# Bias rows by DMA broadcast, the index table first on Pool, and a later third batch, in a fused Fourier-mixing and channel-mix kernel

## The chip, the cores and the metric

One core of one Trainium2 chip. The metric is the device time of one execution in microseconds (us). All runs told of here are in the same, fast state (granted clock 0.995 to 1.0). In the views PE is TensorE and PEld its weight loads, DVE is VectorE, ACT is ScalarE, POOL is GpSimd, and SPq marks a DMA that SyncE issues; a bracket at the end of a line gives the engine's wait before it and what ended that wait. "Ratio" always means the mean time of one kernel's fast runs over the mean of the other's of the same rounds, so it is not quite the ratio of the medians quoted beside it; the brackets are 95% intervals.

## The reference

```python
def _attn_ref(x, w_r, w_i, b_r, b_i):          # x: (8, 3072, 256)
    X = np.fft.rfft(x, axis=1); Xr, Xi = X.real, X.imag
    Yr = Xr @ w_r - Xi @ w_i + b_r             # complex linear layer with a bias
    Yi = Xr @ w_i + Xi @ w_r + b_i
    Y  = soft_threshold(Yr, 0.01) + 1j * soft_threshold(Yi, 0.01)
    return np.fft.irfft(Y, n=3072, axis=1)

def _moe_ref(x, mu_k, mu_r, w_k, w_v, w_r):    # on the result of the first
    x_prev = x moved on by one token
    xk = mu_k * x + (1 - mu_k) * x_prev;  xr = mu_r * x + (1 - mu_r) * x_prev
    k = np.maximum(xk @ w_k, 0);  v = (k * k) @ w_v
    return sigmoid(xr @ w_r) * v
```

## The kernel before

The transform of 3072 points is split as 96 x 32, and both halves are matmuls with tables of sines that the kernel makes itself at the start (`FT`, `FI`, `G`, `GI`). A batch goes through these stages. Line numbers are those of the kernel before; in the changed kernel most are 8 to 25 lower.

- **First** transforms, L280: x against `FT`; the result goes to DRAM (`Adr`, L291) and comes back in another layout as `A` (L305). The first two batches go another way, with x turned by transposes instead (L335, L353).
- **Middle**: second transforms (L378 for group 0, L395), the complex linear layer (L423), bias and threshold on DVE and ACT, then back with `GI` (L462). The result goes to DRAM (`Vdr`, L475) and comes back as `V` (L486).
- **Last** transforms, L543: `V` against `FI`. Then the token tiles: relu units L635, gates L662, output L679.

A small scheduler in the kernel's own Python code lays the work of all batches out in one order. Every unit has a `due` time, and estimates of when its inputs are ready; of the units that are ready, the one with the lowest due time goes next to TensorE (PE).

The start:

```python
    bb, bsel = ...                                  # zeroed on DVE
    load_x(0, 0)
    bbf = ...                                       # two small loads of b_r, b_i
    nc.gpsimd.iota(n1c, ...)
    seli = scs[0:2, 600:856]...
    nc.gpsimd.iota(seli, ...)                       # L87, 2 x 256 elements
    ...                                             # bsel, bb from seli, bbf on DVE
    nc.gpsimd.iota(fmul, ...)                       # L110
    for q in range(1, 4):
        load_x(0, q)                                # L68, also on Pool (gpsimd)
    ...                                             # FT; four iotas n2c; ident
    nc.gpsimd.iota(qk, pattern=[[1, NG], [96, 32]], ...)   # L143, 128 x 768
    nc.vector.tensor_scalar(out=qk, in0=qk, scalar1=j24, scalar2=n2c, ...)  # L153
    ...                                             # 7 us of DVE work: the angles of G
    wr = load_w("wr", w_r, NCD, D)
    wi = load_w("wi", w_i, NCD, D)
```

The bias rows, spread over the partitions by two matmuls and five copies:

```python
    def table_bias(ps, h, end):
        nc.tensor.matmul(ps[:, 0:512], bsel[:, 0, :], bb.rearrange("p a d -> p (a d)"), ...)
        nc.tensor.matmul(ps[:, 512:768], bsel[:, 1, :], bb[:, 0, :], ...)
        def evac(k):
            for t_, lo in ((bias, 0), (bias, 512), (bias0, 512)):
                nc.scalar.activation(t_[:, lo:lo + 512], ps[:, 0:512], AF.Copy, ...)
            nc.scalar.activation(bias0[:, 0:256], ps[:, 512:768], AF.Copy, ...)
            nc.scalar.activation(bias0[:, 256:512], ps[:, 0:256], AF.Copy, ...)
```

The due times (P = 71.5 us is a batch's period; the code counts batches from 0, the text from one, so `b == 2` is the third batch):

```python
        else:                                       # batches 2 to 7
            fb += first(b, s - 0.9 * P, s - 0.2 * P)
            fa += middle(b, s, s + 0.5 * P)
            fc += last(b, s + 0.75 * P, s + 0.95 * P)
```

Of the kernel before, what the change touches and what calls it, by code (L numbers as in the profile page):

```python
# [22 lines left out]
def kernel(  # L23
# [41 lines left out]
    def load_x(b, q):  # L65
# [5 lines left out]
    bb = const.tile([128, 2, D], BF16, name="bb")  # L71
    bsel = const.tile([128, 2, 128], BF16, name="bsel")
    nc.vector.memset(bb, 0.0)
    nc.vector.memset(bsel, 0.0)
    load_x(0, 0)
    bbf = const.tile([2, D], FP32, name="bbf")
    nc.sync.dma_start(out=bbf[0:1, :], in_=b_r.rearrange("(o d) -> o d", o=1))
    nc.sync.dma_start(out=bbf[1:2, :], in_=b_i.rearrange("(o d) -> o d", o=1))
# [7 lines left out]
    seli = scs[0:2, 600:856].rearrange("p (a c r) -> p a c r", a=2, c=2)  # L86
    nc.gpsimd.iota(seli, pattern=[[0, 2], [1, 2], [0, 64]], base=0, channel_multiplier=1,  # L87
                   allow_small_or_imprecise_dtypes=True)
# [13 lines left out]
    for i in range(2):  # L102
        nc.vector.tensor_copy(out=bb[0:2, i, :], in_=bbf)

    nc.vector.tensor_scalar(out=bsel[0:2].rearrange("p a (c r) -> p a c r", c=2), in0=seli, scalar1=1.0,
                            scalar2=None, op0=ALU.not_equal)
    nc.vector.tensor_copy(out=bsel[0:2, 1, 64:65], in_=bsel[0:2, 1, 0:1])

# [3 lines left out]
    for q in range(1, 4):  # L112
        load_x(0, q)
# [17 lines left out]
    for r in range(4):  # L131
# [5 lines left out]
        nc.vector.memset(sc1[sl], float(2 * PI / N) if r % 2 == 1 else 0.0)  # L137
    ident = const.tile([128, 128], FP16, name="ident")
# [3 lines left out]
    qk = scr[:, 0:768].rearrange("p (g k) -> p g k", k=32)  # L142
    nc.gpsimd.iota(qk, pattern=[[1, NG], [96, 32]], base=0, channel_multiplier=0,  # L143
                   allow_small_or_imprecise_dtypes=True)
# [10 lines left out]
    for c in range(2):  # L155
# [8 lines left out]
    hk = scs[:, 500:516]  # L164
    nc.gpsimd.iota(hk, pattern=[[96, 16]], base=48, channel_multiplier=0,
                   allow_small_or_imprecise_dtypes=True)
# [24 lines left out]
    wi = load_w("wi", w_i, NCD, D)  # L191
    muk = const.tile([128, NCD], FP32, name="muk")
# [12 lines left out]
    free = {"pe": 0.0, "act": 6.0, "dve": 13.3}  # L205
# [537 lines left out]
    bias = const.tile([128, 1024], BF16, name="bias")  # L743
    bias0 = const.tile([128, 1024], BF16, name="bias0")

    def table_bias(ps, h, end):
        nc.tensor.matmul(ps[:, 0:512], bsel[:, 0, :], bb.rearrange("p a d -> p (a d)"), start=True, stop=True)
        nc.tensor.matmul(ps[:, 512:768], bsel[:, 1, :], bb[:, 0, :], start=True, stop=True)

        def evac(k):  # L750
            for t_, lo in ((bias, 0), (bias, 512), (bias0, 512)):
                nc.scalar.activation(t_[:, lo:lo + 512], ps[:, 0:512], AF.Copy, bias=0.0, scale=1.0)
            nc.scalar.activation(bias0[:, 0:256], ps[:, 512:768], AF.Copy, bias=0.0, scale=1.0)
            nc.scalar.activation(bias0[:, 256:512], ps[:, 0:256], AF.Copy, bias=0.0, scale=1.0)
            done["bias"] = run_on("act", k, 2.6)
            release(h, done["bias"])

        at(end, evac)

# [9 lines left out]
    P = 71.5  # L769
    START = 50.0  # L770
    tok, val, fa, fb, fc, tab = [], [], [], [], [], []
    for b in range(B):
# [5 lines left out]
        elif b == 1:  # L778
            fb += direct(b, 35.0, 36.0, 50.0)
            fa += middle(b, 41.0, 65.0)  # L780
            fc += last(b, s + 0.75 * P, s + 0.95 * P)
        else:
            fb += first(b, s - 0.9 * P, s - 0.2 * P)
            fa += middle(b, s, s + 0.5 * P)
            fc += last(b, s + 0.75 * P, s + 0.95 * P)
# [26 lines left out]
    done["FT"] = 5.0  # L812
    at(13.3, tables)
# [59 lines left out]
```

## Time and profile before

| | before |
|---|---|
| device time, median of 3 (range) | 595.51 us (595.29 to 595.68) |
| span of the profiled execution | 593.3 us |
| PE busy | 566.7 us, 96% |
| first L423 | 21.65 us |
| L378 of batches 2, 3, 4, 5 | 45.48, 120.91, 190.80, 261.68 us |

Second, two windows of the kernel before (window, length, then busy us of PE, PEld, DVE, ACT, POOL, the granted clock, DMA share, GB/s). The second is the worst of the steady state: 1.4 of 10 us are lost on PE.

```profile
120.00:130.00 10.00, 9.86 (x81) 7.33 (x81) 9.18 (x16) 6.77 (x8) 0.00 (x0) 1.00 0.20 54
...
250.00:260.00 10.00, 8.60 (x107) 6.84 (x106) 7.04 (x16) 6.44 (x8) 0.00 (x0) 1.00 0.81 243
```

The full timeline of that stretch, still before, says why: the last transforms of the fourth batch wait for `V`, which was stored from 234.18 us and asked for again only at 243.09.

```profile
234.18 3.48 SPq L475 DMA_DIRECT2D Vdr<-V  x4
...
243.09 1.91 SPq L486 DMA_DIRECT2D V<-Vdr  x4
...
251.19 0.34 PE L543 MATMUL banks<-FI,V 96*128 96x96 f16 x4 [0.39 <-DMA V<-Vdr]
...
252.49 1.02 PE L543 MATMUL banks<-FI,V 96*128 96x96 f16 x20 [0.96 <-DMA V<-Vdr]
```

### The profile page before, as it was taken

The page shows a single profiled execution, that of the slowest core. Times are in us where ns is not written, and L with a number is a line of the kernel's source. Part 1 is how long each engine was busy: PE and PEld are TensorE (multiplying, and loading weights), DVE is VectorE, ACT ScalarE, POOL GpSimd, SP SyncE. Part 2 cuts the span into 40 slices and gives each one's busy share as a digit, 9 for nine tenths or more (in the row PEclk, how much of TensorE's full clock was granted, in tenths as well). Part 3 has the DMA queues.
Part 4 walks back from the last instruction along what each step waited for, and adds up shares of the span by engine and source line. Part 5 has one row for each costly group of instructions (what it writes and reads, how often), then busy time and mean ns, then how long its engine had stood idle before and what let it go on. Part 6 is the DMA issues. An engine that isn't in the chain of part 4 may idle for free.

```text
span 593.3 us, 12315 instructions
## 1 busy us (share of the span) xinstructions
PE 566.7 (96%) x4824; PEld 428.9 (72%) x4891; DVE 519.3 (88%) x834; ACT 425.5 (72%) x467; POOL 23.5 (4%) x53
## 2 busy tenths in 40 slices
PE   4989999999999999999999999999999999999996
PEld 3878666777767787677777777677876787776665
DVE  7788999789998899888998989988999889979883
ACT  6887967677768677676777677777776867766652
POOL 7001000000000000000000000000000000000000
PEclk9999999999999999999999999999999999999999
DMA  8936888624599256773478655683338722362223
GB/s 150 167 80 158 186 193 226 178 72 104 129 225 237 60 139 140 204 225 67 116 167 245 154 120 129 165 238 106 100 93 235 178 55 73 103 164 72 68 57 90
DMA packets 68878, 84.06 MB, mean 142 GB/s; under 512 B 9042, under 2 KB 53844, under 8 KB 68820
## 3 DMA queue, kind: packets, MB, share of 16 engines
q1 hardware_dynamic: 62916, 68.98, 41.7%
q0 software_dynamic: 5712, 14.03, 15.1%
q8 instruction: 38, 0.62, 0.4%
q10 hardware_dynamic: 192, 0.26, 0.2%
q14 instruction: 20, 0.16, 0.1%
HBM read 50.07 MB, written 47.19 MB: 164 GB/s over the span
## 4 chain that ended last, share of the span: by engine, by line
PE 81%; ACT 7%; DVE 4%; DMA 3%; issue 2%; SPq 1%; POOL 0%; POOLq 0%; DVEq 0%; ACTq 0%
PE banks L679 27%; PE banks L635 23%; PE banks L423 14%; PE banks L662 5%; PE banks L462 3%; PE banks L280 3%; PE banks L395 3%; ACT rl L641 2%; PE banks L543 2%; ACT rg L667 1%; DMA xs<-in_x_dram 1%; DMA Adr<-A 1%; ACT YT L227 1%; PE banks L353 1%; SPq L305 1%
## 5 line engine op out<-in xcount | busy, mean ns | idle before, releaser
L641 ACT ACTIVATE rl<-banks 128x1024 bf16<-128x1024 f32 x192 | 193.5, 1028 | 94.0 <-PE banks L635 88.2
L635 PE MATMUL banks<-xk,wk 128*128 128x512 bf16 x701 | 188.7, 379 | 5.3 <-DVE xk L608 0.7
L679 PE MATMUL banks<-wv,k 128*128 128x256 bf16 x1536 | 183.0, 272 | 0.4 <-ACT rl L641 0.3
L679 PEld LDWEIGHTS <-k 128*128 128x128 bf16 x1536 | 149.3, 98 | 29.1 <-issue 1.4
L647 DVE TENSOR_TENSOR k<-rl 128x1024 bf16<-128x1024 bf16 x192 | 130.3, 684 | 13.3 <-ACT rl L641 13.3
L635 PEld LDWEIGHTS <-wk 128*128 128x128 bf16 x768 | 73.9, 98 | 60.7 <-issue 3.1
L423 PEld LDWEIGHTS <-XT 128*128 128x128 bf16 x768 | 74.5, 98 | 16.4 <-issue 0.9
L423 PE MATMUL banks<-wr,XT 128*128 128x256 bf16 x384 | 73.3, 272 | 0.6 <-ACT A L227 0.2
L423 PE MATMUL banks<-wi,XT 128*128 128x256 bf16 x384 | 73.3, 273 | 0.0
L608 DVE SCALAR_TENSOR_TENSOR xk<-diff,muk,YT 128x512 bf16<-128x512 bf16 x96 | 69.1, 744 | 0.2
L608 DVE SCALAR_TENSOR_TENSOR xr<-diff,mur,YT 128x512 bf16<-128x512 bf16 x96 | 68.7, 744 | 0.0
L690 DVE TENSOR_TENSOR o<-banks,rg 128x1024 f32<-128x1024 f32 (+1 forms) x49 | 58.6, 1196 | 3.7 <-PE banks L679 3.4
L227 ACT ACTIVATE YT<-banks 128x768 bf16<-128x768 f32 x59 | 44.9, 827 | 12.1 <-PE banks L543 9.1
L662 PE MATMUL banks<-wrm,xr 128*128 128x256 bf16 x384 | 49.8, 272 | 0.1
L227 ACT ACTIVATE XT<-banks 128x1024 bf16<-128x1024 f32 (+2 forms) x45 | 42.8, 956 | 9.2 <-PE banks L395 8.4
L667 ACT ACTIVATE rg<-banks 128x1024 bf16<-128x1024 f32 x48 | 49.1, 1024 | 0.0
L227 ACT ACTIVATE A<-banks 96x1024 bf16<-96x1024 f32 (+1 forms) x41 | 41.3, 1022 | 8.0 <-PE banks L280 6.2
L440 ACT ACTIVATE z<-banks 128x1024 bf16<-128x1024 f32 x32 | 32.7, 1022 | 19.9 <-PE banks L423 19.8
L662 PEld LDWEIGHTS <-xr 128*128 128x128 bf16 x384 | 37.2, 98 | 11.6 <-issue 0.2
L227 ACT ACTIVATE V<-banks 128x1024 bf16<-128x1024 f32 x35 | 35.9, 1024 | 11.6 <-PE banks L462 10.6
L602 DVE TENSOR_TENSOR diff<-YT 128x1024 bf16<-128x1024 bf16 x48 | 32.8, 683 | 3.8 <-ACT YT L227 3.8
L452 DVE TENSOR_TENSOR Y<-z,Y 128x1024 bf16<-128x1024 bf16 x48 | 33.2, 693 | 1.7
(101 smaller groups left out, 437.1 us busy)
## 6 DMA issues: line engine op xcount, KB each, us to landing
out_dram<-o SPq DMA_DIRECT2D x188, 128.0 KB, 2.3
xs<-in_x_dram POOLq DMA_DIRECT2D x32, 384.0 KB, 6.2
Vdr<-V SPq DMA_DIRECT2D x192, 64.0 KB, 1.8
V<-Vdr SPq DMA_DIRECT2D x32, 384.0 KB, 6.3
Adr<-A SPq DMA_DIRECT2D x24, 384.0 KB, 5.3
A<-Adr SPq DMA_DIRECT2D x48, 192.0 KB, 4.5
wk<-in_moe_w_k_dram POOLq DMA_DIRECT2D x1, 512.0 KB, 11.7
wv<-in_moe_w_v_dram POOLq DMA_DIRECT2D x1, 512.0 KB, 13.5
```

Of the source, the lines that this page charges most:

```text
L227: nc.scalar.activation(out, in_, AF.Copy, bias=0.0, scale=1.0)
L423: nc.tensor.matmul(o, lhs, w[:, c, :], start=(w is wr and c == 0), stop=(w is wi and c == NCD - 1))
L452: nc.vector.tensor_tensor(out=y, in0=z, in1=y, op=ALU.subtract)
L602: nc.vector.tensor_tensor(out=df, in0=y, in1=yp, op=ALU.subtract)
L608: nc.vector.scalar_tensor_tensor(out=m[:, c, :], in0=df[:, c, :], scalar=mu[:, c:c + 1], in1=yp[:, c, :], op0=ALU.mult, op1=ALU.add)
L635: nc.tensor.matmul(ps[:, 512 * f:512 * f + 512], wk[:, c, 128 * ff:128 * ff + 128], xk[:, c, :], start=(c == 0), stop=(c == NCD - 1))
L641: nc.scalar.activation(rl, ps, AF.Relu, bias=0.0, scale=1.0)
L647: nc.vector.tensor_tensor(out=k2, in0=rl, in1=rl, op=ALU.mult)
L662: nc.tensor.matmul(ps[:, 256 * q:256 * q + 256], xr[:, c, 128 * q:128 * q + 128], wrm[:, c, :], start=(c == 0), stop=(c == NCD - 1))
L667: nc.scalar.activation(rg, ps, AF.Sigmoid, bias=0.0, scale=1.0)
L679: nc.tensor.matmul(ps[:, 256 * q:256 * q + 256], K2[t][:, ff, 128 * q:128 * q + 128], wv[:, ff, :], start=(ff == 0), stop=(ff == NCF - 1))
L690: nc.vector.tensor_tensor(out=o[:, lo:hi], in0=ps[:, lo:hi], in1=rg[:, lo:hi], op=ALU.mult)
```

## The change

Three parts, each meant to win PE idle time:

1. The bias rows are spread by four DMAs with a repeated source, which removes the matmuls, the copies, an iota and the DVE work.
2. The index table `qk` is made on Pool right after the first two loads of x, so that the angle table on DVE, and with it the Sin passes on ACT, begin earlier. The scheduler's constants follow.
3. The first transforms of the third batch get later due times, nearer to their use.

```diff
-    bb = const.tile([128, 2, D], BF16, name="bb")          # and bsel, bbf, the DVE work on them
-    seli = scs[0:2, 600:856].rearrange("p (a c r) -> p a c r", a=2, c=2)
-    nc.gpsimd.iota(seli, pattern=[[0, 2], [1, 2], [0, 64]], ...)
 ...
-    for q in range(1, 4):
+    load_x(0, 1)
+    qk = scr[:, 0:768].rearrange("p (g k) -> p g k", k=32)
+    nc.gpsimd.iota(qk, pattern=[[1, NG], [96, 32]], ...)    # moved up; hk is moved up too
+    for q in range(2, 4):
         load_x(0, q)
 ...
+    bias5 = const.tile([128, 5, D], BF16, name="bias5")     # after wr, wi
+    for src, p0, p1, g0, g1 in ((b_r, 0, 64, 0, 5), (b_i, 64, 128, 1, 5),
+                                (b_i, 65, 128, 0, 1), (b_r, 64, 65, 0, 1)):
+        nc.gpsimd.dma_start(out=bias5[p0:p1, g0:g1, :],
+                            in_=src.rearrange("(o a d) -> o a d", o=1, a=1)
+                                   .to_broadcast([p1 - p0, g1 - g0, D]))
+    bias0 = bias5[:, 0:4, :]...;  bias = bias5[:, 1:5, :]...
 ...
-    free = {"pe": 0.0, "act": 6.0, "dve": 13.3}
+    free = {"pe": 0.0, "act": 6.0, "dve": 12.0}
 ...
-    def table_bias(ps, h, end): ...                         # whole function
 ...
-            fb += first(b, s - 0.9 * P, s - 0.2 * P)
+            fb += first(b, s - (0.5 if b == 2 else 0.9) * P, s - (0.1 if b == 2 else 0.2) * P)
 ...
-    done["FT"] = 5.0
-    at(13.3, tables)
-    tab = [Unit(6.0, 0.6, [], table_bias), Unit(18.0, 0.1, ["FT"], table_fi)]
+    done["FT"], done["bias"] = 5.0, 21.0
+    at(12.0, tables)
+    tab = [Unit(18.0, 0.1, ["FT"], table_fi)]
```

More of the change, by code (lines that the diff above doesn't have):

```diff
@@ L69, in load_x @@
         xs[b, q] = t
-    bb = const.tile([128, 2, D], BF16, name="bb")
-    bsel = const.tile([128, 2, 128], BF16, name="bsel")
-    nc.vector.memset(bb, 0.0)
-    nc.vector.memset(bsel, 0.0)
     load_x(0, 0)
-    bbf = const.tile([2, D], FP32, name="bbf")
-    nc.sync.dma_start(out=bbf[0:1, :], in_=b_r.rearrange("(o d) -> o d", o=1))
-    nc.sync.dma_start(out=bbf[1:2, :], in_=b_i.rearrange("(o d) -> o d", o=1))
     n1c = const.tile([128, 1], FP32, name="n1c")
@@ L84 @@
     scs = k2_pool.tile([128, 2048], FP32, name="k2")
-    seli = scs[0:2, 600:856].rearrange("p (a c r) -> p a c r", a=2, c=2)
-    nc.gpsimd.iota(seli, pattern=[[0, 2], [1, 2], [0, 64]], base=0, channel_multiplier=1,
-                   allow_small_or_imprecise_dtypes=True)
     warm = const.tile([128, 1], FP32, name="warm")
@@ L99, in reduce_angle @@
         nc.vector.tensor_tensor(out=m, in0=m, in1=r, op=ALU.add)
-    for i in range(2):
-        nc.vector.tensor_copy(out=bb[0:2, i, :], in_=bbf)
-    nc.vector.tensor_scalar(out=bsel[0:2].rearrange("p a (c r) -> p a c r", c=2), in0=seli, scalar1=1.0,
-                            scalar2=None, op0=ALU.not_equal)
-    nc.vector.tensor_copy(out=bsel[0:2, 1, 64:65], in_=bsel[0:2, 1, 0:1])
     fmul = scs[:N1, 0:96]
@@ L111 @@
                    allow_small_or_imprecise_dtypes=True)
-    for q in range(1, 4):
+    load_x(0, 1)
+    qk = scr[:, 0:768].rearrange("p (g k) -> p g k", k=32)
+    nc.gpsimd.iota(qk, pattern=[[1, NG], [96, 32]], base=0, channel_multiplier=0,
+                   allow_small_or_imprecise_dtypes=True)
+    for q in range(2, 4):
         load_x(0, q)
@@ L137 @@
         nc.vector.memset(sc1[sl], float(2 * PI / N) if r % 2 == 1 else 0.0)
+    hk = scs[:, 500:516]
+    nc.gpsimd.iota(hk, pattern=[[96, 16]], base=48, channel_multiplier=0,
+                   allow_small_or_imprecise_dtypes=True)
     ident = const.tile([128, 128], FP16, name="ident")
     make_identity(nc, ident)
-    qk = scr[:, 0:768].rearrange("p (g k) -> p g k", k=32)
-    nc.gpsimd.iota(qk, pattern=[[1, NG], [96, 32]], base=0, channel_multiplier=0,
-                   allow_small_or_imprecise_dtypes=True)
     ph = scs[:, 400:464].rearrange("p (c k) -> p c k", c=2)
@@ L163 @@
     nc.vector.memset(ang[64:96, 0, :, 0:16], 0.0)
-    hk = scs[:, 500:516]
-    nc.gpsimd.iota(hk, pattern=[[96, 16]], base=48, channel_multiplier=0,
-                   allow_small_or_imprecise_dtypes=True)
     for c in range(2):
@@ L191 @@
     wi = load_w("wi", w_i, NCD, D)
+    bias5 = const.tile([128, 5, D], BF16, name="bias5")
+    for src, p0, p1, g0, g1 in ((b_r, 0, 64, 0, 5), (b_i, 64, 128, 1, 5), (b_i, 65, 128, 0, 1), (b_r, 64, 65, 0, 1)):
+        nc.gpsimd.dma_start(out=bias5[p0:p1, g0:g1, :],
+                            in_=src.rearrange("(o a d) -> o a d", o=1, a=1).to_broadcast([p1 - p0, g1 - g0, D]))
+    bias0 = bias5[:, 0:4, :].rearrange("p g d -> p (g d)")
+    bias = bias5[:, 1:5, :].rearrange("p g d -> p (g d)")
     muk = const.tile([128, NCD], FP32, name="muk")
@@ L741, in table_gi @@
         return issue
-    bias = const.tile([128, 1024], BF16, name="bias")
-    bias0 = const.tile([128, 1024], BF16, name="bias0")
-    def table_bias(ps, h, end):
-        nc.tensor.matmul(ps[:, 0:512], bsel[:, 0, :], bb.rearrange("p a d -> p (a d)"), start=True, stop=True)
-        nc.tensor.matmul(ps[:, 512:768], bsel[:, 1, :], bb[:, 0, :], start=True, stop=True)
-        def evac(k):
-            for t_, lo in ((bias, 0), (bias, 512), (bias0, 512)):
-                nc.scalar.activation(t_[:, lo:lo + 512], ps[:, 0:512], AF.Copy, bias=0.0, scale=1.0)
-            nc.scalar.activation(bias0[:, 0:256], ps[:, 512:768], AF.Copy, bias=0.0, scale=1.0)
-            nc.scalar.activation(bias0[:, 256:512], ps[:, 0:256], AF.Copy, bias=0.0, scale=1.0)
-            done["bias"] = run_on("act", k, 2.6)
-            release(h, done["bias"])
-        at(end, evac)
     def tables(k):
```

## The prediction

> **What bounds the kernel now.** I read the page's busy shares first, then the busy time by windows of 10 us, then the timeline of the first 30 us, and last the queue and timeline around the third batch's first transforms.
>
> ```profile
> PE 566.7 (96%) x4824; PEld 428.9 (72%) x4891; DVE 519.3 (88%) x834; ACT 425.5 (72%) x467; POOL 23.5 (4%) x53
> ...
> 0.00:10.00 10.00, 3.20 (x28) 2.30 (x29) 6.45 (x41) 5.10 (x10) 8.22 (x24) 1.00 0.75 123
> 10.00:20.00 10.00, 8.12 (x90) 7.18 (x89) 6.91 (x10) 9.10 (x11) 2.80 (x4) 1.00 1.13 210
> 20.00:30.00 10.00, 9.88 (x122) 8.95 (x120) 8.33 (x15) 8.02 (x9) 0.00 (x0) 1.00 0.83 137
> ...
> 90.00:100.00 10.00, 9.89 (x67) 6.66 (x67) 9.69 (x14) 6.67 (x8) 1.01 (x2) 1.00 0.96 230
> 100.00:110.00 10.00, 9.75 (x91) 7.22 (x89) 9.02 (x17) 6.63 (x8) 0.00 (x0) 1.00 0.71 185
> 110.00:120.00 10.00, 9.41 (x94) 7.06 (x95) 6.68 (x12) 7.50 (x10) 0.00 (x0) 1.00 0.57 159
> ```
>
> In the window lines the columns are the window, its length, then busy us of PE, PEld, DVE, ACT and POOL, the granted clock, the DMA share and GB/s. PE is busy 566.7 of 593.3 us, at full clock. So only 26.6 us of the span are PE idle time, and a change that leaves PE's work alone can win only some of those. They lie at the two ends: 6.8 us in 0 to 10, 1.9 in 10 to 20, and about 5.4 after 580. From 20 to 130 us the windows give 6.0 us of idle time; later the batches repeat with 0.05 to 0.3 us in most windows. What happens after 130 us is set by PE and comes out as a plain shift of what happened before.
>
> Now the start, from the timeline (start, length, engine, line, operation, with the wait before it in brackets):
>
> ```profile
> 4.90 1.54 ACT L752 ACTIVATE bias<-banks 128x512 bf16<-128x512 f32 x3
> ...
> 5.36 0.89 POOL L143 IOTA YT<- 128x768 f32 x1
> ...
> 6.28 0.68 DVE L153 TENSOR_SCALAR YT<-YT,j,n2c 128x768 f32<-128x768 f32 x1 [0.86 <-POOL YT L143]
> ...
> 13.07 1.25 PEld L335 LDWEIGHTS <-xs 96*128 96x128 bf16 x16 [0.62 <-DMA xs<-in_x_dram]
> ...
> 13.46 1.57 ACT L761 ACTIVATE G<-YT,sc 128x1536 f16<-128x1536 f32 x1
> ...
> 15.62 1.58 ACT L175 ACTIVATE G<-YT,sc 128x1536 f16<-128x1536 f32 x1
> 15.79 2.97 PEld L353 LDWEIGHTS <-YT 128*128 128x128 bf16 x31 [0.60 <-ACT YT L227]
> ```
>
> Two chains meet here. One is the angle table: iota on POOL, seven microseconds of DVE work (6.28 to 13.41), two Sin passes on ACT. The other is x: its four quarters land at about 6.1, 9.3, 11.2 and 13.07, which the waits of L335 show. The bias work (two matmuls, 0.6 us at 3.2 us, and five ACT copies, 4.90 to 6.98) stands in the gap while PE waits for x anyway.
>
> **What the Trainium skill says.** (1) "Perfetto Trace Analysis", section "Identifying the Most-Contended Engine", warns that matmul occupancy is no good measure of distance to the roofline, because matmuls are pipelined, and asks for the weight loads' share as well. Here that is 72%; but the chain of waits is 81% PE and the gaps between matmuls are all but gone, so for the order question PE's idle time is still the budget. (2) "DMA: Bandwidth & Descriptors", section "Issuing engines are not separate DMA queues", says that transfers of all issuing engines end on the same 16 engines and interleave. The trace agrees: the DMA share is 1.13 from 10 to 20 us, while the POOL queue alone is feeding x and the weights, so later bytes wait behind earlier ones. (3) The same page, "Anatomy of one DMA — SWDGE (gpsimd) path", gives about 2.0 us plus bytes over 436e3 per us. For a quarter of x (786 KB read as fp32) this is 3.8 us as an estimate; the first one was issued by 1.88 us and used at 6.16, 4.3 us later. It fits roughly. (4) The same page, "Rules for kernel authors", allows a DMA source to repeat (a broadcast), and warns only of repeats in the destination; no trace before shows such a broadcast.
>
> **Part 1: bias by DMA.** Removed: 2 matmuls and their 2 weight loads, 5 ACT copies (1.54 + 0.38 + 0.39 = 2.3 us), on DVE two memsets, two casts and two small operations (0.27 + 0.17 + 0.48 + 0.28 + 0.14 = 1.3 us), one iota (0.36 us) on POOL and two small loads. All of it lies before 7 us, where PE waits for x: nothing is won on PE directly. Added: four issues on POOL behind wi. Those of wr and wi took 0.82 and 0.73 us, so I take 0.75 us for the two large and 0.5 for the two small ones, 2.5 us. They delay the issue of the second batch's x by that, and of wk, which landed at 8.9 + 11.7 = 20.6 us and is first used at 65. The rows are 64*5 + 64*4 + 63 + 1 = 640 of 512 bytes; wr or wi has 256 such rows and landed some 0.6 us after the one before it. So 640 rows take about 1.6 us and land at about 14.3 + 1.6 = 16, or 20 if rereading one row is three times slower. The first addition of a bias was at 23.7. So this is hidden: 0.
>
> **Part 2: table first on POOL.** The index table (0.89 us) moves ahead of two x loads and the small iotas. L153 then waits for the last of four small iotas instead: 1.95 us to 2.2 (two small iotas), load to 2.7, table to 3.6, two loads to 4.6, four iotas to 5.3. So DVE's seven microseconds run from 5.34 to 12.5, 0.9 us earlier, and the Sin passes from 12.5 to 15.6 without the copy between them, 1.6 us earlier than 17.2. But the built order of the engines shows what pays for it: ACT now does both passes before its copy of the last quarter of x, DVE does its last such copy only after the four small operations on G (15.65 to 16.1), and PE has 16 transposes of G ahead of the transposes of x. So the copies of the last x quarter end at 15.6 + 0.8 = 16.4 on ACT and 16.1 + 0.95 = 17.05 on DVE, against 15.74 before; the x transposes begin near 17.1 instead of 15.1 to 15.8. All the GI transposes and the last two x transposes are however done before the first L423. Following the evacuations one by one (ACT: two GI copies to 18.35, two A copies to 20.25, XT to 21.1; DVE: two A copies to 20.2, two XT copies to 22.1, the sign turn to 22.4), I get the first L423 at about 22.2, against 21.65 before. It has about 0.6 us more PE work behind it than before (the moved transposes, less the 0.3 us of bias matmuls). The two cancel to within my error. Fewer evacuations remain in the 20 to 40 us stretch, which had 0.95 us of PE idle time; I credit 0.4 us in all. Start: -0.4 us.
>
> **Part 3: third batch later.** Against the text of the change, the built PE order differs little: the first six of its eight units stay where they were, because PE had nothing better ready. The last two move back by about 8 and 16 us of PE work, and the second batch's last transforms (L543) come forward by up to 9 us. From the seventh token tile's last relu unit on, the order is the same as before to the end. So only 93 to 125 us are touched, and the idle time there is 0.05 + 0.05 + 0.25 + 0.47 + 0.12 + 0.08 = 1.0 us in six windows of 5 us. Spreading L543 should take away most of the stretch around 110 us: -0.6 us. Against it stands a new nearness, in these lines:
>
> ```profile
> 93.09 1.46 PE L280 MATMUL banks<-xs,FT 96*96 96x512 bf16 x6
> ...
> 95.05 1.57 SPq L291 DMA_DIRECT2D Adr<-A  x2
> ...
> 104.61 3.90 SPq L305 DMA_DIRECT2D A<-Adr  x8
> ...
> 120.91 0.38 PE L378 MATMUL banks<-G,A 128*128 128x256 f16 x2
> ```
>
> The last unit's result goes through DRAM (L291 out, L305 back) before L378 can use it. From the last unit (94.1) to L378 there were 27 us; in the new order there are 12.3 us of PE work, with small gaps 12.8. The chain: evacuation done 2.0 us after the unit starts; landing 4 to 8 us (3.9 and 6.5 for two single stores at 75 and 79 us, 7.9 for the wait at 104.6, when two stores and two x loads ran together), I take 5.7; the first four reads 1.4 us to issue and 3.5 to land; 0.3 for hand-overs. That is 12.9 us: just about no wait, but each extra microsecond of landing is one of PE idle time. I put 0.6 us on it as a mean over landings of 5 to 8 us.
>
> **Sum.** 595.5 - 0.4 - 0.6 + 0.6 = 595.1 us.
>
> **Rivals.** (a) The DRAM round trip becomes a PE wait: landing at 8 us and x loads beside it give 2 to 3 us, so about 597.5. For it: the longest wait of L305 was 7.9 us. Against it: only one store and one x load now run together, and the last batch's, with no x load, took 5.2. (b) The start is really faster: if the copies of x find ACT and DVE free earlier than I traced, the 1.6 us won on the Sin passes reach PE, and with the relief at 110 us it is about 593. For it: the chain of waits runs through both Sin passes and x. Against it: x still lands at 13.07. (c) L543 now comes at about 93.7 us and its loads were issued from 84.83 to 86.56; loads of this kind landed in 6.3 us at the median, up to 8.6, so a wait of up to 1 us may arise: 596. (d) The broadcast is slow and the first bias addition waits: a few microseconds; it would need a rate four times below that of wr.
>
> **Range and chances.** The terms spread about 0.7 us (start), 0.4 (relief) and 1.2 (round trip) either way; the runs before spread 0.4 us. Together about 2 us either way: 593.1 to 597.1. Two per cent is 11.9 us, more than the PE idle time from 10 to 130 us, so faster by that gets 0.01; slower by it needs a transfer late by over 10 us, 0.01 too.
>
> **What would show it.** Right: bias landed before 20 us with no wait of the first bias addition; the first Sin at about 12.5 and the second done at 15.6; first L423 between 21.6 and 22.6; PE idle time of about half a microsecond at 110 us less; L378 of the third batch at 123 us with a wait under 1.5 us; every event after 130 us shifted by one constant. Wrong: a wait of L378 of over 3 us, L423 under 21, or a shift that changes later on.

## More of the kernel before

L378 is issued once per batch, so its eight start times are milestones; the distance between two of them says how much a stretch of the program cost.

The prediction shows the page, the start and the third batch. Two further places matter for the argument. First, the Pool timeline of the kernel before (start, length, engine, line, operation): the iota for the bias stands just ahead of the loads of x.

```profile
2.04 0.36 POOL L87 IOTA k<- 2x256 f32 x1
...
2.52 1.54 POOL L68 DMA_DIRECT2D xs<-in_x_dram  x3
```

## The result, and the profile after

| | before | changed |
|---|---|---|
| device time, median of 4 (range) | 595.40 us (594.63 to 595.68) | 593.72 us (592.58 to 593.95) |
| ratio | | 0.997 [0.9953, 0.9987] |
| span of the profiled execution | 593.3 us | 591.9 us |
| PE idle in the span | 26.6 us | 26.7 us |

The result is right to the reference and 1.7 us faster: "within 2%", and inside the range. The page after opens so:

```profile
PE 565.2 (95%) x4823; PEld 428.7 (72%) x4889; DVE 524.1 (89%) x832; ACT 419.3 (71%) x457; POOL 26.5 (4%) x56
```

PE's idle time is the same as before; its busy time is 1.5 us less, though only four instructions left it. The ends of matmuls are modelled in a trace and some of their records can be missing, so I do not build on that row. (These two profiles hold 4824 and 4823 matmuls for 4891 and 4889 weight loads; the other twelve have as many matmuls as weight loads, and 21.3 to 23.9 us of PE idle time. So the 26.6 us are some 3 us too many.) The milestones are better evidence. Changed minus before, in us:

| | L378 of batch 2 | L378 of batch 3 | L378 of batch 4 | L378 of batch 5 | L543 at 529 us | end |
|---|---|---|---|---|---|---|
| before | 45.48 | 120.91 | 190.80 | 261.68 | 529.08 | 593.3 |
| changed | 44.76 | 124.02 | 191.07 | 260.66 | 528.08 | 591.9 |
| shift | -0.72 | (moved in the order) | +0.27 | -1.02 | -1.00 | -1.4 |

So 0.7 us are won at the start, 1.0 is lost again between batches 2 and 4, 1.3 are won between batches 4 and 5, and the shift then stays to 529 us. (The last 0.4 us appear in the final token tiles; I did not follow them.) The parts, one by one:

**The start.** From the whole timeline of the changed kernel:

```profile
2.22 0.55 POOL L68 DMA_DIRECT2D xs<-in_x_dram  x1
...
5.35 0.74 DVE L140 TENSOR_SCALAR YT<-YT,j,n2c 128x768 f32<-128x768 f32 x1 [0.33 <-POOL n2c L120]
...
12.64 1.57 ACT L736 ACTIVATE G<-YT,sc 128x1536 f16<-128x1536 f32 x1 [1.30 <-DVE YT L89]
...
15.73 1.89 PE L717 MATMUL banks<-ident,G 128*128 128x128 f16 x16 [1.58 <-ACT G L159]
...
22.86 0.38 PE L415 MATMUL banks<-wr,XT 128*128 128x256 bf16 x2
```

The angle work begins at 5.35 instead of 6.28 and the first Sin at 12.64 instead of 13.46. PE is now ready for `G` and waits 1.58 us for it, and the first linear-layer matmul (L415, formerly L423) is *later*, 22.86 against 21.65. Since all the GI transposes have been done by then, less is left to do: from this matmul to the second batch's L378 it is 21.90 us, before 23.83. So L378 is 0.7 us earlier, and the later first matmul was no loss here.

**The bias.** From the same timeline, the last of the four broadcast issues and the first addition of a bias:

```profile
9.91 0.99 POOL L180 DMA_DIRECT2D bias<-in_b_r_dram  x1
...
24.80 1.23 DVE L427 TENSOR_TENSOR z<-banks,bias 128x1024 bf16<-128x1024 f32 x1 [0.39 <-PE banks L415]
```

By the list of DMA issues, the first broadcast (160 KB) landed 8.7 us after its issue at 7.66, so at about 16.4 us, and the last (0.5 KB, one partition) 11.9 us after 9.91, so near 22. Both are in time: the addition waits 0.39 us for PE, not for a DMA.

**The third batch.** Windows after (before is in the prediction and above):

```profile
90.00:100.00 10.00, 9.80 (x81) 7.04 (x81) 9.68 (x19) 6.96 (x8) 0.51 (x1) 1.00 0.87 221
100.00:110.00 10.00, 9.83 (x78) 6.87 (x78) 8.98 (x13) 7.17 (x9) 0.00 (x0) 1.00 0.24 63
110.00:120.00 10.00, 9.95 (x93) 7.18 (x93) 8.56 (x13) 8.08 (x11) 0.51 (x1) 1.00 0.62 141
120.00:130.00 10.00, 8.23 (x73) 6.51 (x73) 6.66 (x11) 5.91 (x7) 0.00 (x0) 1.00 0.82 195
...
250.00:260.00 10.00, 9.71 (x116) 7.77 (x116) 8.24 (x17) 7.51 (x10) 0.00 (x0) 1.00 0.72 189
```

From 100 to 120 us PE gains 0.08 + 0.54 us, as the change intends. From 120 to 130 it loses 1.63: the loss comes from one wait, in the timeline after.

```profile
109.89 0.60 PE L272 MATMUL banks<-xs,FT 96*96 96x512 bf16 x2
...
111.81 0.31 SPq L283 DMA_DIRECT2D Adr<-A  x1
...
118.20 3.91 SPq L297 DMA_DIRECT2D A<-Adr  x8
...
124.02 0.38 PE L370 MATMUL banks<-G,A 128*128 128x256 f16 x2 [1.72 <-DMA A<-Adr]
```

The last first-transform is now at 109.89 instead of 94.1. Its store is issued at 111.81, the reads at 118.20, and L370 (formerly L378), which would have been ready at 122.3, waits 1.72 us for them.

**The fourth batch's V.** The last line of the windows shows 1.11 us of PE work more than before from 250 to 260 us, in a place that no part of the change touches. The timeline of the changed kernel:

```profile
234.46 1.88 SPq L467 DMA_DIRECT2D Vdr<-V  x4
...
239.14 2.72 SPq L478 DMA_DIRECT2D V<-Vdr  x4
...
250.57 1.19 PE L535 MATMUL banks<-FI,V 96*128 96x96 f16 x24
```

The stores of `V` begin at the same place in the order, but the reload follows 4.7 us after them instead of 8.9, because the stores land in 2.6 us at the median instead of 5.4 (list of DMA issues, 234 to 243 us). The last of the four decides: it landed 3.13 us after its issue, before 7.35, and the reload was issued 0.1 us after that in both. The waits of 0.39 and 0.96 us on PE are gone. (The expectations below speak of the fifth batch here; counted from one, it is the fourth.) Whether this is the change's doing, or luck, is the main question for the experiments.

### The profile page after: what moved, and what is told of

It is laid out like the page before. It is cut to its first block, busy times and chain, and to the rows that moved or that the text cites. A ratio compares the mean times of both kernels' runs of the same rounds, so it can differ in the third digit from the quotient of the medians.

```text
span 591.9 us, 12302 instructions
## 1 busy us (share of the span) xinstructions
PE 565.2 (95%) x4823; PEld 428.7 (72%) x4889; DVE 524.1 (89%) x832; ACT 419.3 (71%) x457; POOL 26.5 (4%) x56
## 4 chain that ended last, share of the span: by engine, by line
PE 83%; ACT 7%; DVE 4%; issue 2%; DMA 2%; POOL 1%; SPq 0%; POOLq 0%; ACTq 0%; DVEq 0%
PE banks L671 28%; PE banks L627 23%; PE banks L415 14%; PE banks L654 5%; PE banks L454 4%; ACT rl L633 3%; PE banks L387 3%; PE banks L272 3%; PE banks L535 2%; ACT rg L659 2%; DMA Adr<-A 1%; DVE A L221 1%; DMA A<-Adr 1%; DVE z L427 1%; ACT A L219 1%
## 5 line engine op out<-in xcount | busy, mean ns | idle before, releaser
L639 DVE TENSOR_TENSOR k<-rl 128x1024 bf16<-128x1024 bf16 x192 | 130.5, 685 | 13.3 <-ACT rl L633 13.2
L415 PEld LDWEIGHTS <-XT 128*128 128x128 bf16 x768 | 74.5, 98 | 15.5 <-DVE XT L397 0.3
L415 PE MATMUL banks<-wi,XT 128*128 128x256 bf16 x384 | 73.3, 273 | 0.0
L415 PE MATMUL banks<-wr,XT 128*128 128x256 bf16 x384 | 73.3, 272 | 0.0
L219 ACT ACTIVATE XT<-banks 128x1024 bf16<-128x1024 f32 (+2 forms) x46 | 43.2, 949 | 12.5 <-PE banks L387 9.8
L219 ACT ACTIVATE YT<-banks 128x768 bf16<-128x768 f32 x57 | 43.5, 832 | 11.8 <-PE banks L535 8.9
L219 ACT ACTIVATE A<-banks 96x1024 bf16<-96x1024 f32 (+1 forms) x38 | 38.3, 1022 | 7.4 <-PE banks L272 6.9
L221 DVE CAST A<-banks 96x1024 bf16<-96x1024 f32 (+1 forms) x22 | 26.7, 1220 | 10.1 <-PE banks L272 9.8
```

The lines of the kernel that those rows point to most:

```text
L219: nc.scalar.activation(out, in_, AF.Copy, bias=0.0, scale=1.0)
L221: nc.vector.tensor_copy(out=out, in_=in_)
L415: nc.tensor.matmul(o, lhs, w[:, c, :], start=(w is wr and c == 0), stop=(w is wi and c == NCD - 1))
L639: nc.vector.tensor_tensor(out=k2, in0=rl, in1=rl, op=ALU.mult)
```

## The experiments

Twelve runs, in three groups of four; the kernels of a group ran on one chip, with shared runs of the kernel before. Three rounds or more are needed, since differences of 1 us (0.17%) are at issue. Three theories about the 1.7 us stand against each other:

- The start makes the gain, by part 1, by part 2 or by both.
- The third batch's new order makes it (or its wait eats what the start wins).
- The gain falls near 250 us, where the timing of the `V` stores against something else decides.

### Group one: how steady are the two, and which part is it?

**The kernel before again, unchanged.**

> The kernel before, unchanged, profiled once more. In its first profile the shift between the two kernels was +0.27 us (the changed kernel later) from batch 3 up to 250 us, and turned to -1.0 us only because L543 of the fifth batch waited 1.35 us for loads of V there. Theory A (the gain of the whole is chance of DMA: a late store of V in the fifth batch that comes and goes): in this new profile the wait at 250 us is absent or elsewhere, and the times of this kernel against itself are 1.000 but spread by about 1 us. Theory B (it belongs to this kernel's order): the wait of 0.96 + 0.39 us stands again at 250 us, all times at about 595.3.

Measured: 594.91 us (593.94 to 596.46), ratio 0.9994 [0.9975, 1.0013]. In its profile L543 waits for `V` for 0.95 + 0.54 us near 250 us, and once more, 0.54 us, at 323. The wait is thus a habit of this kernel. Its time scatters more than the first three runs showed: the group's runs of the kernel before lie between 593.99 and 597.63.

**The changed kernel again, unchanged.**

> The changed kernel, unchanged, profiled once more. Both theories: the wait of the third batch's first L378 line (L370 here) for the read back from DRAM is there again, 1.2 to 2.2 us, and the start is 0.8 us ahead at 93 us. Theory A: a wait for V somewhere in a later batch is as likely as in the kernel before. Theory B: none, ratio to before 0.997.

Measured: 592.67 us (592.21 to 593.25), ratio 0.9956 [0.9937, 0.9974]. The gain is real, 2.2 to 2.3 us here. This time L370 of the third batch has no wait of 0.5 us or more, so the 1.72 us of the first profile is not a constant. There is no wait for `V` near 250.

**The changed kernel with the third batch's old due times** (parts 1 and 2 alone).

```diff
-            fb += first(b, s - (0.5 if b == 2 else 0.9) * P, s - (0.1 if b == 2 else 0.2) * P)
+            fb += first(b, s - 0.9 * P, s - 0.2 * P)
```

> Changed kernel with the third batch's first transforms put back to their old due times (parts 1 and 2 alone). From the traces: part 1 and 2 are worth 0.8 us at 93 us, the third batch cost 1.07 us after that, so this should be 0.8 us under before up to 250 us and 1.1 us under the changed kernel there. Theory A: ratio to before 0.9975 to 0.999 or so, whatever the wait at 250 us does. Theory B (that wait belongs to the third batch's order): the wait of 1.3 us at 250 us stays, 594.6 us, slower than the changed kernel by about 0.9.

Measured: 593.15 us (592.51 to 593.44), ratio 0.9961 [0.9942, 0.9979]. Without part 3 nearly the whole gain is there. No wait for `V` near 250. That is neither theory's case: B wanted the wait, A a ratio of 0.9975 or more.

**The kernel before with part 3 alone.**

```diff
-            fb += first(b, s - 0.9 * P, s - 0.2 * P)
+            fb += first(b, s - (0.5 if b == 2 else 0.9) * P, s - (0.1 if b == 2 else 0.2) * P)
```

> The kernel before with the third batch's first transforms alone ordered later. From the traces: 1.07 us later than before between 130 and 250 us, with a wait of 1.2 to 2.2 us of the third batch's L378 for A. Theory A: 596.4 us, less or more by the V wait's chance. Theory B: the V wait of 1.3 us at 250 us is gone, so 595.1, equal to before within 0.3 us.

Measured: 595.45 us (593.85 to 597.47), ratio 1.0003 [0.9979, 1.0026]: nothing, between the 596.4 of theory A and the 595.1 of B. The waits of PE in its profile show both costs side by side:

```profile
PE banks L378 <- DMA A<-Adr: 1.2, 1, 1.2
...
PE banks L543 <- DMA V<-Vdr: 0.8, 1, 0.8
```

(waited for: us in total, times, longest). So part 3 alone neither wins nor removes the wait for `V`. With these profiles part 3 can be measured by itself, as the distance from L378 of batch 2 to L378 of batch 4:

| kernel | distance, us | of it, wait of L378 for A | rest |
|---|---|---|---|
| before; before again; start only | 145.32; 145.33; 145.52 | none | 145.3 to 145.5 |
| changed | 146.31 | 1.72 | 144.59 |
| part 3 only | 145.87 | 1.19 | 144.68 |
| changed again | 144.53 | none | 144.53 |

The new order relieves PE by 0.77 us (144.60, the mean over the four profiles with the new order, that of the changed kernel plus four PE instructions told of below included, against 145.37 over the seven with the old order), and gives it back as a wait for `A` that has another size in each run.

### Group two: parts 1 and 2 apart, part 3 milder, and a test of the 250 us place

What might decide how fast the `V` stores land? Between 234 and 243 us the traces show much the same kinds of transfer in both kernels: stores of `V` in 512-byte packets, loads of x, a store of `A`, outputs. One thing that stands out is a single packet on q8, the queue that the page calls "instruction": 16,384 bytes, at 235.6 us before and at 236.2 us after, 1.42 and 1.78 us after the first `V` store. The Trainium skill ("Runtime: NRT & Kernel Launch", section "Instruction fetch mechanics") says that an engine's program is refilled in 16 KiB blocks by the sequencer's own DMA queue, and calls the cost mostly hidden. With the 64 bytes per instruction of "Perfetto Trace Analysis" (section "The 4-stage abstract model"), PE's 4824 + 4891 counted instructions would be 622 KB, as an estimate; q8 moved 38 packets, 0.62 MB. So these packets are very likely PE's program. Part 1 takes four instructions out of PE's program before that point, which could shift where a block ends. The theory that follows: four dummy instructions put back would bring the wait for `V` back.

**The changed kernel plus four PE instructions** (two small matmuls with their weight loads, in a PSUM area that is overwritten right after; at 5 us, where PE is idle).

```diff
     def table_fi(ps, h, end):
+        for _ in range(2):
+            nc.tensor.matmul(ps[:96, 0:96], FT, FT, start=True, stop=True)
         nc.tensor.matmul(ps[:96, 0:96], FT, ident[:96, :96], start=True, stop=True)
```

> The changed kernel with four more PE instructions at the start (two matmuls of 96x96 and their weight loads, written over by the third; they run while PE waits for ident and x, so they cost no time there). Seen so far: the wait of L543 for V in the fifth batch stands in every profile with the old start (1.35, 1.49 and 0.79 us) and in none with the new one (three profiles), whatever the third batch does. Theory C: the new start has four PE instructions fewer, so PE's instruction fetch of 16 KB near 236 us comes some 0.4 us later against the stores of V and no longer holds up the last of them; with the four instructions put back the wait at 250 us returns, 0.5 to 1.5 us, and the kernel loses that against the changed one. Theory D: it is something else in the new start (the addresses of buffers, the POOL queue's transfers); no wait, same time as the changed kernel.

Measured: 597.23 us (594.9 to 598.61), ratio 1.0049 [1.0018, 1.008]: 4.6 us more than the changed kernel's 592.67 of the group before (and 4.8 more than the milder version's 592.44 in the same group), for instructions that cost nothing where they stand (L378 of batch 2 at 45.34 us, against 44.76 and 45.37 in the changed kernel). The timeline of this run:

```profile
234.08 3.48 SPq L467 DMA_DIRECT2D Vdr<-V  x4
...
243.15 1.98 SPq L478 DMA_DIRECT2D V<-Vdr  x4
...
251.91 0.34 PE L535 MATMUL banks<-FI,V 96*128 96x96 f16 x4 [1.20 <-DMA V<-Vdr]
...
253.20 1.02 PE L535 MATMUL banks<-FI,V 96*128 96x96 f16 x20 [0.95 <-DMA V<-Vdr]
```

The old picture is back, reload 9.1 us after the stores, waits of 1.20 and 0.95 us, and the program packet is again 1.45 us after the first store. The profiled execution was the fastest of the four (594.9); the others took up to 3.7 us more, so the executions without a profile must lose time in places that this trace does not show.

**The kernel before with part 1 alone.** The edit is the diff of part 1 above, nothing else.

> The kernel before with the biases by DMA alone: table order as before; PE order as before less the two bias matmuls. Theory C: four PE instructions fewer, so no wait of L543 for V at 250 us; 1.3 us gained there; the start itself gains nothing (L378 of batch 2 at 45.5 to 46.1). Theory D with addresses or the POOL queue: no wait either. If the wait stands, both C and D fall as far as they lay it on the bias part.

Measured: 593.41 us (592.78 to 593.76), ratio 0.9976 [0.9955, 0.9997]. Part 1 alone gives most of the gain. L378 of batch 2 is at 45.05, where 45.5 to 46.1 had been expected, the reload of `V` 4.4 us after the stores, no wait.

**The kernel before with part 2 alone.** The edit is the diff of part 2 above: `qk` and `hk` moved up, 13.3 made 12.0.

> The kernel before with the index table first and its scheduler's times moved (12.0 for 13.3), bias still by matmul. L378 of batch 2 at about 45 us, that is 0.7 us ahead of before, if the table part makes the start's gain; at 45.8 if that gain needs ACT free of the bias copies. Theory C: as many PE instructions as before, though in another order, so the wait for V at 250 us stands, 0.5 to 1.5 us.

Measured: 594.85 us (594.34 to 595.19), ratio 1.0001 [0.998, 1.0021]. It brings nothing: the first L423 (L424 here) is at 24.54 and L378 of batch 2 at 46.44, 0.6 us later than the mean of 45.81 with the old start. The index table is early, but not what should follow from it:

```profile
3.06 0.90 POOL L114 IOTA YT<- 128x768 f32 x1
...
6.61 0.77 DVE L157 TENSOR_SCALAR YT<-YT,j,n2c 128x768 f32<-128x768 f32 x1
...
13.75 1.57 ACT L762 ACTIVATE G<-YT,sc 128x1536 f16<-128x1536 f32 x1 [2.62 <-DVE YT L99]
```

The angle work begins at 6.61 (before 6.28, changed 5.35) and the first Sin at 13.75 (before 13.46, changed 12.64). DVE still has the bias work ahead of it here, and its two casts of the bias rows (L103), which ran beside Pool's x load and table iota, took 0.68 and 1.02 us where they took 0.28 each before. So this run shows part 2 beside the bias work, and not what part 2 does in the changed kernel.

**The changed kernel with a milder part 3.**

```diff
-            fb += first(b, s - (0.5 if b == 2 else 0.9) * P, s - (0.1 if b == 2 else 0.2) * P)
+            fb += first(b, s - (0.5 if b == 2 else 0.9) * P, s - (0.2 if b == 2 else 0.2) * P)
```

> The changed kernel with the third batch's first transforms ending at 0.2 P ahead of its use for 0.1 P: the last one comes 8 us of PE work earlier, the second batch's L543 still spread out. If the relief is worth 1.0 us and the wait for A (1.72, 1.19 and 0 us in three profiles) takes it back, this keeps the relief without the wait: L378 of the third batch to that of the second 74.4 us apart where start_only has 75.6 and before 75.4, no wait for A, and the time 0.3 to 1.0 us under the changed kernel.

Measured: 592.44 us (592.42 to 594.07), ratio 0.9967 [0.9944, 0.9991]. The distance of batch 2 to batch 4 is 145.05 us with no wait for `A`: 0.3 us won in place of 0.77 won and up to 1.72 given back. (From batch 2 to batch 3 it is 75.0 us, not the 74.4 expected.)

### Group three: does the instruction count really set it, and what in part 1 makes the start faster?

**Part 1 alone plus the same four PE instructions.** This is the sharper test: its PE instruction count is that of the kernel before.

```diff
     def table_fi(ps, h, end):
+        for _ in range(2):
+            nc.tensor.matmul(ps[:96, 0:96], FT, FT, start=True, stop=True)
```

> Bias by DMA alone, with four PE instructions put back in PE's idle time at the start (the same two matmuls as in after_pe4). The kernel before and all variants with the old number of PE instructions sent the loads of V in the fifth batch 7.3 to 9.1 us after the last stores of V had begun, those with four fewer 4.4 to 4.8 us. Theory C (the phase of PE's instruction fetch): fetch 1.4 to 1.7 us after the stores began, loads 7 to 9 us after, a wait of L543 at 250 us again; 1 us or more slower than bias_only (0.9976), start as in bias_only. Theory D (addresses, POOL queue): as bias_only.

Measured: 593.75 us (593.03, 594.02, 596.37, 593.48), ratio 0.9985 [0.9961, 1.001]. The wait for `V` is *not* back. The timeline of this run:

```profile
234.01 1.88 SPq L464 DMA_DIRECT2D Vdr<-V  x4
...
238.59 2.59 SPq L475 DMA_DIRECT2D V<-Vdr  x4
```

The program packet comes 2.03 us after the first store, and the reload 4.6 us after it. So the count of PE instructions does not by itself set when the packet comes, and that form of the theory falls. One of its four runs was slow all the same (596.37).

**Part 1 alone with the 2 x 256 iota back on Pool**, its result unused.

```diff
+    seli = scs[0:2, 600:856].rearrange("p (a c r) -> p a c r", a=2, c=2)
+    nc.gpsimd.iota(seli, pattern=[[0, 2], [1, 2], [0, 64]], base=0, channel_multiplier=1,
+                   allow_small_or_imprecise_dtypes=True)
```

> Bias by DMA alone, with the small iota of 2x256 (0.36 us) put back on POOL ahead of the x loads, its result not used. bias_only had x's last quarter at 12.57 us against 12.85 to 13.28 with the old start, and the first L423 at 21.21 against 21.65 to 22.25. Theory E (the start's gain is that POOL issues the x loads 0.3 us earlier): x's last quarter back at 12.9 or later, first L423 at 21.6 or later, L378 of the second batch at 45.5 or later against 45.05. Theory F (the gain is ACT and DVE free of the bias copies): stays at 21.2 and 45.1. Under C there is no wait for V at 250 us in either case.

Measured: 594.22 us (593.93 to 594.51), ratio 0.9986 [0.9964, 1.0009]. L378 of batch 2 is at 46.47, against 45.05 without the iota: the start's gain is gone, and more than that, for 46.47 is later than all three profiles with the old start (45.48 to 46.08). Theory E's three marks are met and F's are not, but by one profile. Pool's timeline of this run shows the iota where it was, and the loads of x behind it at 2.54:

```profile
2.06 0.36 POOL L80 IOTA k<- 2x256 f32 x1
...
2.54 1.55 POOL L68 DMA_DIRECT2D xs<-in_x_dram  x3
```

The last quarter of x is used at 13.62 us here, at 12.57 with part 1 alone, at 13.08 before. (The second load of x was issued when it was before, 2.54 against 2.52, and landed 0.55 us later, so some of the 13.62 is scatter of the transfers.) There is one wait for `V` of 0.37 us near 250 us, though the program packet comes at 1.75 us and the reload 4.4 us after the stores.

**Part 1 with the milder part 3**, without part 2.

```diff
-            fb += first(b, s - 0.9 * P, s - 0.2 * P)
+            fb += first(b, s - (0.5 if b == 2 else 0.9) * P, s - 0.2 * P)
```

> Candidate for the best: bias by DMA, the old table order, and the third batch's first transforms in the milder order (0.5 P to 0.2 P ahead). bias_only gives 45.05 for L378 of the second batch, third_milder 145.05 from there to that of the fourth (bias_only 145.33): 0.3 us under bias_only, no wait for V, so ratio to before 0.9965 to 0.9975.

Measured: 593.42 us (593.21 to 593.75), ratio 0.9972 [0.9957, 0.9988], as expected, though L378 of batch 2 came at 45.77 and not at 45.05.

**The changed kernel with the milder part 3, again.**

> third_milder once more, beside bias_third: the changed start with the milder third batch. If the table order neither wins nor loses (start_only 45.11, bias_only 45.05 at L378 of the second batch), both agree within 0.4 us; if the table first loses its 0.6 us also here (table_only was 0.6 us behind before), bias_third is ahead by that.

Measured: 592.69 us (592.14 to 593.16), ratio 0.9959 [0.9944, 0.9975]. With 0.9967 before, against 0.997 and 0.9956 of the changed kernel, the milder version is as good as the changed one and not measurably better.

This pair is also the test of part 2 that the expectation asked for, and it missed: the two do not agree within 0.4 us. On the same chip in the same rounds, the six executions with the table first took 592.14 to 593.16 us (mean 592.67), the six with the old table order 593.21 to 593.75 (mean 593.45). So with part 1 (and the milder part 3) in place, the table first is worth about 0.8 us, by this one pair of kernels, though alone it was worth nothing. Where, the profiles do not show in full: L378 of batch 2 is 0.26 us apart (45.51 and 45.77), and the two profiled executions only 0.16 us (593.16 and 593.32).

### What the fourteen profiles say together

For each profile I took the time from the first `V` store of this stretch (near 234 us) to the program packet on q8, to the reload of `V`, and the distance from L378 of batch 4 to L378 of batch 5.

| kernel | packet, us after the first store | reload, us after the first store | waits of the last transforms for V near 250 us | L378 of batch 4 to 5 |
|---|---|---|---|---|
| before | 1.42 | 8.91 | 0.39 + 0.96 | 70.88 |
| before again | 1.65 | 8.84 | 0.95 + 0.54 | 71.02 |
| part 3 only | 1.46 | 8.26 | 0.79 | 70.45 |
| part 2 only | 1.46 | 7.29 | none | 69.58 |
| changed + 4 PE | 1.45 | 9.07 | 1.20 + 0.95 | 71.70 |
| changed; changed again | 1.78; 1.81 | 4.68; 4.42 | none | 69.59; 69.58 |
| start only | 2.14 | 4.78 | none | 69.58 |
| part 1 only; + 4 PE; + iota | 1.83; 2.03; 1.75 | 4.38; 4.58; 4.38 | none; none; 0.37 | 69.58; 69.58; 69.73 |
| part 1 + milder part 3 | 1.99 | 4.80 | none | 69.58 |
| milder; again | 1.85; 1.77 | 4.55; 4.40 | none | 69.58; 69.58 |

The split is clean: packet at 1.65 us or earlier, reload 7.3 to 9.1 us after the stores; packet at 1.75 or later, 4.4 to 4.8. One experiment (four instructions more) moved both together, and one (the same four, on part 1 alone) moved neither.

The kept traces say how the two hang together. In before, part 3 only, part 2 only and changed + 4 PE, the packet begins within 0.05 us of the moment at which SyncE begins to issue the last of the four `V` stores. That one issue then takes 2.05, 1.62, 1.33 and 2.05 us and ends 0.2 to 0.4 us after the packet; in the nine profiles with an early reload the packet begins 0.33 to 0.70 us after the issue does, and the issue takes 0.44 or 0.45 us. This is the difference between the store rows shown above, 3.48 us before and 1.88 changed. Pool's load of x, issued 0.35 to 0.40 us after the last store began, moves most of its packets before those of the held-up store, and that store lands 5.75 to 7.52 us after its issue instead of 2.84 to 3.28. Before again is different: its packet began 0.23 us into the issue, which was not longer (0.45 us), but a few packets of the stores came late and it landed after 7.29 us.

The same coincidence stands everywhere in the fourteen traces. Of 365 DMA issues of SyncE after 30 us that began while a packet of q8 was in flight, or up to 0.2 us ahead of one, 208 took over 0.75 us, and all 208 ended 0.15 to 0.40 us after the packet; of the other 6431, 73 took that long (their median is 0.42 us). So it is read from the traces, though not forced by an edit, that a packet of q8 goes with a held-up issue on SyncE, and that this makes the store late. What sets the packet's time against the stores stays open: no experiment moved it at will.

## Why the prediction was right or wrong

The total was right (595.1 predicted, range to 593.1; measured 593.72). The sum behind it was not. Against the means over the profiles:

| term | predicted | measured |
|---|---|---|
| start (L378 of batch 2) | -0.4 | -0.67 (45.81 over three profiles with the old start, 45.14 over six with the new) |
| relief of PE around 110 us | -0.6 | -0.77 |
| wait for A of the third batch | +0.6 | 0, 0.76, 1.19, 1.72: mean +0.92 |
| waits for V near 250 us | no such term | -1.2 (mean 70.78 over the three kernels with the old start that wait, 69.58 without) |
| sum | -0.4 | -1.7 |

The measured sum agrees with the first comparison (-1.7); the second gave -2.3. The closeness is in part chance, as the wait for A alone ranges over 1.72 us. The V term is the one that separates prediction and result, and that the total still fell inside the range is luck as far as this term goes.

- **The bound** was read rightly: PE's order and its few idle microseconds. The change stayed far inside 2%. Its budget of 26.6 us was some 3 us too large, for the missing records told of above.
- **Part 1, "nothing is won on PE directly", is the step that failed in the start's term.** The PE and ACT work removed was indeed hidden. But the iota removed from Pool stood ahead of the issue of x: 2.52 before, 2.22 after. Part 1 alone moves batch 2's L378 from 45.81 (mean) to 45.05, 45.30 and 45.77 in three profiles, and with the iota put back it is 46.47. I had the iota's 0.36 us in the list and saw only PE. The amount scatters as much as it is large: 0.3 us in the issue, 0.04 to 0.8 at the mark. Part 2 alone issues the second load as late as before and has x's last quarter at 12.54 anyway, so the issue time is not the only thing that moves it. That Pool's queue makes this gain is therefore likely and not shown beyond doubt.
- **Part 2** ran as worked out on its own engines (DVE at 5.35 for 5.34 predicted, first Sin at 12.64 for 12.5, second done at 15.68 for 15.6), and as feared it pays elsewhere: first L423 at 22.86 to 23.60 in the six profiles of the changed start, above the 21.6 to 22.6 that I had named. Both sides of the sum were mis-sized. Against the three profiles with the old start the first L423 came 1.26 us later (23.24 against 21.98, 0.55 predicted), and the stretch from there to L378 of batch 2 was 1.93 us shorter (21.90 against 23.83, in every one of these profiles; 0.6 predicted). Of the -0.67, the three profiles with part 1 and the old table order have -0.44 (45.37). That the two effects cancel does not hold for the executions: on top of part 1 the table first was worth about 0.8 us. The ratio of 1.0001 for part 2 alone does not bear on it, as the Sin pass was not early there.
- **Part 3**: relief and wait were both named, each too small, and they cancel as predicted (-0.77 + 0.92 = +0.15). Rival (a) did come, but smaller than its 2 to 3 us: 1.72 at most. L378 came at 124.02 rather than 123.
- **"Every event after 130 us shifted by one constant" was false.** The shift is +0.27 at 191 us and -1.02 at 261. I had counted PE's idle time only up to 130 us and called the rest plain repetition, "0.05 to 0.3 us in most windows"; the 1.4 us at 250 to 260 were in the profile before, with the name of the wait on them. What failed is the claim that nothing after 130 us depends on the start: the landing of a store near 240 us does differ between kernels that differ in the start alone (7.35 and 7.29 us before, 2.84 with part 1 alone). The text named "a shift that changes later on" as a sign of error, and that sign is what led to the wait for `V`.
- **Bias broadcast**: landing predicted at 16, or 20 if reading one row is slow; it was 16.4 for the first and 20.5 to 21.8 for the others (the last: 9.91 + 11.9). So the sign "before 20 us" failed, but all were in time for 24.8. The issues cost Pool 0.74 + 1.56 + 0.99 = 3.3 us, not 2.5. Rivals (c) and (d) did not occur.

What stays open: why executions of the kernel before scatter over 593.7 to 597.6 us and those with the changed start mostly over 592.1 to 594.1; the profile of one execution cannot tell. The four extra instructions gave the widest and slowest runs in the changed kernel (up to 598.6) and one such run (596.4) on part 1 alone.

## What to carry to other kernels

Set matched events of the two traces side by side over the whole span before crediting a gain to a part: here the parts that were meant to win (table order, later batch) came to zero each when alone (1.0001 and 1.0003), and most of the gain came with the part that was credited with nothing: most likely from 0.3 us on a queue ahead of x, and from a store 200 us later that lands sooner. Test a part on top of the others as well as alone: the table order was worth nothing beside the old bias work and about 0.8 us without it. Putting a transfer "just in time" buys a steady, small relief (0.77 us) with a wait that is different in every run (0 to 1.72 us); leaving some slack bought less (0.3 us) without the wait. And look for waits on DMA in the profile before in *all* windows, not only where the change works: those are the places that a shift of half a microsecond can open or close.

## What the Trainium skill lacked or had wrong

- "Runtime: NRT & Kernel Launch" calls the refill of an engine's program mostly hidden. The views here put no wait of PE down to it, which agrees; but the page says nothing on its neighbours. In 14 profiles, 208 of the 365 DMA issues of SyncE that began beside a packet of q8 took over 0.75 us, against 73 of 6431 others, and the last store of a group landed 5.75 to 7.52 us after its issue where it was held up, 2.84 to 3.28 us where the packet came 0.33 us or more into the issue. Seen in traces, not forced by an edit.
- "DMA: Bandwidth & Descriptors" has no figure for broadcast loads issued on Pool. Here four of them cost Pool 0.74, 0.66 to 0.94 and 0.99 us of issue, the 0.5 KB one as much as the large ones, and they landed 8.7 to 12.6 us after issue, behind x and the weights. The page's 2.0 us plus bytes over 436e3 per us would give 2.4 us for the 160 KB one, as an estimate; the formula has no term for waiting behind other transfers.
- No page tells how far the landing of the same transfer scatters from one execution to the next in a busy kernel: the wait for one read of `A` was 0 and 1.72 us in two profiles of one kernel.
